# Linear attention with a multiplicative FFN on one Trainium2 core: v of batches 0 and 1 cast to bf16 by its loading DMA, and the sum of k for them by small matmuls on two columns of ones

## The chip, the core and the metric

The kernel runs on one NeuronCore of a Trainium2 chip. TensorE (PE) multiplies matrices into PSUM; VectorE (DVE), ScalarE (ACT) and GpSimd (POOL) do the elementwise work; SyncE (SP) and POOL issue the transfers between HBM and the on-chip memory (SBUF), each on its own DMA queue, SP's called q1 and POOL's q0 in the profile. The metric is the device time of one execution in microseconds (us), lower is better, given as the median of several runs.

## The reference

There are 8 batches, 8 heads, 576 positions and a head dimension of 64. Attention is linear: q and k go through phi, k and v are summed over the positions into a 64x64 matrix per head, k alone is summed into a vector, and each q row is multiplied by both. The result, 4608 rows of 512, goes through an FFN of which the two last matrices follow each other with nothing between.

```python
phi = lambda x: np.where(x > 0, x, np.exp(x) - 1.0) + 1.0
q_p, k_p = phi(q), phi(k)
kv  = np.einsum('bhsd,bhse->bhde', k_p, v)
z   = np.sum(k_p, axis=2)
num = np.einsum('bhsd,bhde->bhse', q_p, kv)
den = np.einsum('bhsd,bhd->bhs', q_p, z)[..., None] + 1e-06
x   = (num / den).transpose(0, 2, 1, 3).reshape(4608, 512)
out = ((x @ w1) * (x @ w2) @ w3) @ w_out
```

## The kernel before

**Order.** The whole program is a list of steps written out by hand, the string `ORDER`. Each step is a letter, a batch or chunk number and a part; the steps are issued in that order, and every engine and every queue executes what it got in that order. A `+` after a step moves it to another engine: loads go to POOL's queue instead of SP's, copies to DVE instead of ACT.

**Attention.** Per batch, 512 of the 576 positions are laid out with four positions (`j`) to a partition, in two halves of four heads; the last 64 positions are a tail of their own. Steps `L`, `M`, `N` load a half of k, q and v as f32 into one of 13 shared `ld` buffers (line 95, 512 KB each), `R` loads the tails (line 104). The steps x, y and z (X, Y, Z for q) make phi of k: exp on ACT (line 168), max and add (line 173) and a min (line 198, line 193 for the tail) on DVE. The step `v` casts a half of v to bf16 (line 204) or its tail (line 210). The target of the cast is `vts[b % 2]`, laid out position, head, 65 columns: 64 of v and a last one that holds 1.0, written once by POOL in the steps `I1` and `I2` (line 84). So the step `K` (lines 216 to 235) gets the sum of k with the product: a matmul over two heads has 2 x 65 = 130 moving columns, and there are 16 of them in a batch (line 225), and two more of 260 columns for the tail (line 229), all accumulating in one PSUM bank per head pair. The result is copied to `kv` (line 234). Step `A` multiplies q by it (line 280) and divides (lines 284 to 286); for batches 0 and 1 the transposes of q (`a`, line 257) and of x (`P`, line 301) run on PE, and only the tails of q of these batches go through a DMA transpose (`T1.1`, `T0.1`, line 249, on SP).

**FFN.** The loads of the weights (`B`, `C`, `E`; lines 114, 118, 126) are issued by POOL and cast f32 to bf16 on the way. Since W3 and W_out follow each other, steps `w` and `u` (lines 136 and 143) multiply them into one matrix at the start. After that a chunk of 512 rows is eight `F` steps (lines 322 to 328, 8 matmuls of 512 columns each, ACT copies one product, DVE multiplies it by the other) and four `O` steps (line 479), stored by `S` (line 489).

The part of the order that the change touches is at the start. Steps on v of batches 0 and 1: loads `N0.1+ N0.0+ N1.0+ N1.1+` on POOL; casts `v0.1` on ACT and `v0.0+ v1.0+ v1.1+` on DVE; tails `v0.2+` on DVE and `v1.2` on ACT; then `K0` and `K1+`.

Of the kernel before, what the change touches and what calls it, by code (L numbers as in the profile page):

```python
# [9 lines left out]
BF16 = mybir.dt.bfloat16  # L10
# [3 lines left out]
P = 128  # L14
# [6 lines left out]
def kernel(  # L21
# [11 lines left out]
    nc = tc.nc  # L33
    B, H, S, D = q.shape
# [35 lines left out]
    vts = [wpool.tile([P, NJ, H, E1], BF16, name=f"vt{i}") for i in range(2)]  # L70
# [3 lines left out]
    def copy_of(alt):  # L74
        return (nc.scalar.copy, nc.vector.tensor_copy, nc.gpsimd.tensor_copy)[alt]

    def constants(part, alt):
        if part == 0:
            make_identity(nc, ident)
        else:  # L80
            eng = nc.vector if alt else nc.gpsimd
            for t in (vrs[part - 1], kvs[part - 1]):
                eng.memset(t, 0.0)
            eng.memset(vts[part - 1][..., D:E1], 1.0)
            for g in range(2):
                eng.memset(vrs[part - 1][g * R:(g + 1) * R, :, g, :, D:E1], 1.0)

# [128 lines left out]
    def kv_full(b, alt):  # L216
        kj, kr = ph["k", b]
        vt, vr, kv = vts[b % 2], vrs[b % 2], kvs[b % 2]
        kvp = at_ps.tile([P, 2, NCH], F32, tag="at", name="kvp")
        W = 2 * E1  # L220
        for i in range(2):
            for g in range(2):
                hp = 2 * g + i
                for j in range(NJ):
                    nc.tensor.matmul(kvp[:, i, g * W:(g + 1) * W],  # L225
                                     kj[:, hp, j].rearrange("p u d -> p (u d)"),
                                     vt[:, j, 2 * hp:2 * hp + 2, :].rearrange("p h e -> p (h e)"),
                                     start=(g == 0 and j == 0), stop=False, skip_group_check=True)
            nc.tensor.matmul(kvp[:, i, 0:2 * W], kr[:, i * P:(i + 1) * P],  # L229
                             vr[:, i].rearrange("p g u e -> p (g u e)"),  # L230
                             start=False, stop=True, skip_group_check=True)
        for u in range(2):
            rows = slice(u * D, (u + 1) * D)
            copy_of(alt)(out=kv[rows, :, :, u], in_=kvp[rows, :, 0:2 * W].rearrange(
                "p i (g u e) -> p i g u e", g=2, u=2)[:, :, :, u])
# [283 lines left out]

    ORDER = """  # L520
    M0.0+ Y0.0 C1 E0 M0.1 I0 X0.0 E3 X0.1 L0.0 Y0.1 Z0.0 Z0.1 C0 y0.0 w0+ R0.0 R0.1 x0.0 E4 x0.2 I1
    w3+ L0.1+ x0.1 a0.0+ E1 y0.2 a0.1+ N0.1+ u0.2+ N0.0+ z0.0 R1.1 v0.1 y0.1 w4+ u3.2+ E2 w1+ z0.2
    z0.1 v0.0+ u4.2 E5 L1.0+ E7 v0.2+ E6 K0 M1.0+ M1.1+ w2 A0.3 y1.0 x1.0 L1.1+ u1.2 A0.0 w5 R1.0+
    u2.2+ w6 A0.2 B3.0 P0.3 Y1.0 z1.0 u5.2 I2 B3.1 X1.0 A0.1 w7+ P0.0 X1.1 Y1.1 N1.0+ N1.1+ Z1.0
    u6.2+ x1.2 P0.2+ x1.1 y1.2 P0.1 u7.2 Z1.1 y1.1 z1.1 B1.0 a1.0+ B1.1 v1.0+ B2.0 B2.1 F0.6 B0.0
    v1.1+ z1.2 T1.1 T0.1 v1.2 F0.7 M2.1 a1.1 K1+ F0.2 A1.2 F0.3 A1.3 F0.4 B0.1 A1.0 P1.2 F0.5 P1.3
    L2.1 A1.1 P1.0+ X2.1 R2.0+ h0 h1 A0.4 P1.1+ Y2.1 h2 h3 R3.0+ M3.1 i0 A1.4 M2.0 i1 x2.1 X3.1 Z2.1
    F1.7 F1.6 x2.2 L2.0 y2.1 y2.2 Y2.0 x3.2 R3.1+ X2.0 O0.3 N2.1 x2.0 z2.1 N2.0 y2.0 z2.2 Z2.0 F1.0
    M3.0 R5.0+ y3.2 T2.0 v2.1 L3.0 Y3.1 R2.1+ F1.5 N3.1 v2.0+ z2.0 L3.1 Z3.1 v2.2+ O0.2 F1.2 F1.1
    Y3.0 y5.2 z3.2 K2 F1.4 A2.2 X3.0 F1.3 L4.0 A2.3 x3.0 O0.1 Z3.0 A2.0 x3.1 N3.0 y3.0 O0.0 v3.1  # L530
    S0.1 A2.1 y3.1 R5.1+ z3.0 z3.1 v3.0 v3.2 O1.1+ O1.0 T3.0 D2.0 S0.0 K3 R4.1+ R4.0+ O1.3 A3.0 O1.2
    A3.2 L4.1 v4.2+ F2.6 A3.3 F2.3 N4.1 y4.1 F2.1 M4.0 x4.1 A3.1 x4.0 F2.0 M4.1 y4.2 M6.1 v5.2+ x4.2
    F2.7 Y4.0 D3.0 F2.4 z4.1 X4.1 F2.2 Y4.1 v4.1 S1.0 F2.5 Z4.1 M5.0 N4.0 X4.0 Z4.0 A3.4 z4.2 y4.0
    O2.3 F3.7 M5.1 Y5.0 v4.0 A2.4 F3.6 z4.0 L5.0 T4.0 R6.0+ x5.2 Y5.1 X5.0 F3.1 N5.1 Z5.0 S1.1 O2.2+
    K4 F3.2 M6.0 x6.2 X5.1 A4.2 Z5.1 F3.4 z5.2 F3.5 y5.0 A4.1 F3.0 L5.1 F3.3 N5.0 y5.1 X6.1 y6.2
    O2.1 A4.3 R6.1+ N6.0 S2.1 x5.1 N6.1 v5.0+ T5.0 O2.0 x5.0 v5.1+ A4.0 R7.0+ z5.1 D4.0 z5.0 X6.0
    O3.3 y7.2 O3.2+ K5+ S2.0 L6.0 z6.2 O3.1 A5.2 L6.1 O3.0 A5.1 D1.1 Y6.1 Z6.1 F4.2 A5.0 Y6.0 F4.5
    y6.1 F4.7 v6.0+ x6.1 L7.0 x6.0 M7.0 A5.3 D3.1 x7.0 z6.1 F4.0 v6.1+ v6.2 F4.6 A4.4 Z6.0 F4.1 S3.0
    F4.4 D5.0 A5.4 y6.0 z6.0 F4.3 M7.1 F5.7 x7.2 y7.0 Y7.0 z7.2 L7.1 N7.0 K6+ z7.0 F5.6 F5.0 y7.1
    X7.1 X7.0 Z7.0 F5.5 S3.1 F5.3 Y7.1 T6.0 R7.1+ Z7.1 A6.3 T7.0 F5.1 O4.2 A6.1 x7.1 O4.1 A6.2 N7.1  # L540
    z7.1 F5.4 A6.0 F5.2 v7.1 v7.2+ O4.0 D6.0 D5.1 A6.4 v7.0 O4.3+ S4.1 K7 O5.0 F6.3 S4.0 O5.1 A7.4
    F6.5 F6.4 D7.1 F6.1 A7.3 O5.2 O5.3 A7.1 F6.2 F8.3 A7.0 F8.6 S5.1 F6.6 A7.2 S5.0 F6.0 F6.7 D7.0
    O6.3+ O6.2 O6.1 O6.0+ F7.1 F7.7 F7.2 F8.0 S6.1 F8.7 S6.0 F8.1 F8.5 F7.4 F8.2 F8.4 F7.6 O8.2 F7.5
    H8.2 F7.3 F7.0 O8.3 H8.3 O7.0 O7.1 S7.0 O8.0 O8.1 S8.0 O7.2 H7.2 Q7.3
    """
    GATES = ""
    ctx.enter_context(tc.manual_schedule())
# [8 lines left out]
    def step(s):  # L556
# [106 lines left out]
```

## Time and profile before

| What | Value |
|---|---|
| median of 3 runs | 257.89 us (257.8, 257.89, 259.88) |
| the profiled execution | 259.98 us, of which the profile's span is 256.4 us |
| TensorE clock granted | 0.998 |
| matmuls and weight loads in the records | 1352 and 1368 |
| HBM read and written | 38.80 MB and 9.44 MB |
| casts of v, f32 to bf16, 128x1024 | 8 on ACT at 1050 ns, 8 on DVE at 691 ns (median; 685 to 929) |
| loads of v issued on POOL | 4 of 512 KB, 10.0 us from issue to landing (median) |

The span begins with the first instruction and ends with the last; the profiled execution has 3.6 us beside it. In the profile a line such as `L225 PE MATMUL kvp<-vt,kj` names the source line, the engine, the operation, and the tiles written and read. An idle time in brackets is put down to whatever came last. Matmuls are pipelined: a matmul of 512 columns is listed with 379 ns, but the next one starts 216 ns later, and eight of 130 columns start 56 ns apart (eight in 0.45 us in the chain of waits).

### The profile page before, as it was taken

Reading aid. Unit: us, or ns where it says so; the run is one execution under the profiler, and the core shown is the slowest. Engines: PE = TensorE matmul, PEld = TensorE weight load, DVE = VectorE, ACT = ScalarE, POOL = GpSimd, SP = SyncE. Lnnn points to the kernel's source line nnn. Section 1 sums busy time; section 2 is a strip of 40 time slices with the busy share of each in tenths; the row PEclk is TensorE's granted clock in tenths of the full one; section 3 lists DMA queues with packets and bytes.
Section 4 is the critical chain, followed back from the end, with each engine's and each line's share of the span. In section 5 each row is a group of like instructions: output and inputs, shape, how many; then the busy total and the mean of one; then the engine's idle time right before and its main releaser. Section 6 shows DMA issues by size and latency. Waiting matters only on the chain.

```text
span 256.4 us, 3789 instructions
## 1 busy us (share of the span) xinstructions
PE 231.0 (90%) x1352; PEld 117.0 (46%) x1368; DVE 159.1 (62%) x350; ACT 117.1 (46%) x180; POOL 48.8 (19%) x84
## 2 busy tenths in 40 slices
PE   0087999999999859999999999999999999999994
PEld 0063665554454424445445445444544444444442
DVE  0548589777998525997887899987244642432300
ACT  2404677247756605756553383544423223233231
POOL 8634479364044300410000000000000000000000
PEclk9999999999999999999999999999999999999999
DMA  6999999999999999799999989736710343000144
GB/s 221 211 238 286 306 261 247 204 229 285 307 239 293 220 213 324 187 289 257 310 355 206 292 246 261 196 63 150 230 20 32 134 83 164 0 3 0 41 143 144
DMA packets 63890, 50.57 MB, mean 197 GB/s; under 512 B 33536, under 2 KB 58368, under 8 KB 63872
## 3 DMA queue, kind: packets, MB, share of 16 engines
q1 hardware_dynamic: 54576, 37.10, 57.2%
q0 software_dynamic: 9152, 13.11, 22.9%
q8 instruction: 10, 0.16, 0.3%
q10 hardware_dynamic: 144, 0.13, 0.1%
q14 instruction: 8, 0.07, 0.1%
HBM read 38.80 MB, written 9.44 MB: 188 GB/s over the span
## 4 chain that ended last, share of the span: by engine, by line
PE 68%; DMA 20%; DVE 4%; issue 3%; SPq 1%; POOL 1%; ACT 1%; DVEq 0%; ACTq 0%; POOLq 0%
PE b_ps L322 22%; PE a_ps L322 22%; PE o_ps L479 18%; DMA w3b<-in_moe_w_dram 9%; DMA out_dram<-o_sb 7%; DMA qk32r<-in_k_dram 3%; PE nd L280 3%; PE kvp L225 2%; SPq L311 1%; DVE y L173 1%; PE o_ps L504 1%; DVE vt L204 1%; ACT a_sb L327 1%; PE kvp L229 1%; DVE kj L198 1%
## 5 line engine op out<-in xcount | busy, mean ns | idle before, releaser
L322 PEld LDWEIGHTS <-w_sb 128*128 128x128 bf16 x576 | 55.1, 98 | 62.8 <-issue 1.6
L328 DVE TENSOR_TENSOR ab<-a_sb,b_ps 128x512 bf16<-128x512 f32 x72 | 49.0, 685 | 39.2 <-PE b_ps L322 28.5
L322 PE MATMUL a_ps<-xt,w_sb 128*128 128x512 bf16 x256 | 66.7, 379 | 0.7 <-ACT a_sb L327 0.6
L322 PE MATMUL b_ps<-xt,w_sb 128*128 128x512 bf16 x256 | 66.7, 379 | 0.2 <-ACT a_sb L327 0.2
L327 ACT COPY a_sb<-a_ps 128x512 f32<-128x512 f32 x72 | 41.8, 586 | 53.1 <-PE a_ps L322 48.7
L479 PE MATMUL o_ps<-wf_sb,ab 128*128 128x512 bf16 x267 | 62.7, 379 | 0.8 <-issue 0.2
L479 PEld LDWEIGHTS <-ab 128*128 128x128 bf16 x280 | 26.9, 98 | 29.9
L481 ACT COPY o_sb<-o_ps 128x512 f32<-128x512 f32 x29 | 16.8, 586 | 43.8 <-PE o_ps L479 33.4
L286 DVE TENSOR_TENSOR xn<-nd,r 128x512 bf16<-128x512 f32 x32 | 22.1, 691 | 1.1
L168 ACT ACTIVATE e<-q 128x1024 bf16<-128x1024 f32 x16 | 16.7, 1055 | 9.4 <-DMA q<-in_q_dram 9.4
L168 ACT ACTIVATE e<-k 128x1024 bf16<-128x1024 f32 x16 | 16.6, 1055 | 4.8 <-DMA k<-in_k_dram 4.8
L280 PE MATMUL nd<-kv,qt 128*128 128x130 bf16 (+1 forms) x160 | 15.8, 220 | 3.1 <-DMA qt<-qj 2.6
L280 PEld LDWEIGHTS <-qt 128*128 128x128 bf16 (+1 forms) x160 | 11.3, 99 | 14.4 <-DMA qt<-qj 3.1
L136 PE MATMUL w3p<-ident,w3b 128*128 128x128 bf16 x64 | 5.7, 242 | 13.2 <-DMA w3b<-in_moe_w_dram 13.2
L284 DVE TENSOR_SCALAR r<-nd 128x8 f32<-128x8 f32 (+1 forms) x40 | 6.4, 161 | 16.2 <-PE nd L280 15.8
L173 DVE TENSOR_SCALAR y<-q 128x1024 bf16<-128x1024 f32 x16 | 11.0, 693 | 7.9 <-DMA q<-in_q_dram 7.9
L143 PE MATMUL wf_ps<-wt_sb,w3t 128*128 128x512 bf16 x61 | 14.8, 379 | 0.8 <-DMA wt_sb<-in_moe_w_out_dram 0.7
L104 POOL DMA_DIRECT2D qk32r<-in_q_dram x14 | 9.0, 648 | 19.2 <-ACT a_sb L327 17.9
L225 PE MATMUL kvp<-vt,kj 128*128 128x130 bf16 x128 | 9.8, 219 | 2.8 <-DVE vt L204 2.0
L198 DVE TENSOR_TENSOR qj<-e,y 128x512 bf16<-128x512 bf16 x32 | 11.9, 416 | 0.4 <-ACT e L168 0.3
L204 ACT CAST vt<-v 128x1024 bf16<-128x1024 f32 x8 | 8.4, 1050 | 7.9 <-DMA v<-in_v_dram 7.9
L198 DVE TENSOR_TENSOR kj<-e,y 128x512 bf16<-128x512 bf16 x32 | 11.9, 418 | 0.2
(54 smaller groups left out, 176.4 us busy)
## 6 DMA issues: line engine op xcount, KB each, us to landing
out_dram<-o_sb SPq DMA_DIRECT2D x15, 512.0 KB, 3.5
q<-in_q_dram SPq DMA_DIRECT2D x13, 512.0 KB, 8.5
k<-in_k_dram SPq DMA_DIRECT2D x13, 512.0 KB, 6.5
v<-in_v_dram SPq DMA_DIRECT2D x12, 512.0 KB, 8.1
w3b<-in_moe_w_dram POOLq DMA_DIRECT2D x8, 256.0 KB, 12.1
v<-in_v_dram POOLq DMA_DIRECT2D x4, 512.0 KB, 10.0
w_sb<-in_moe_w_dram POOLq DMA_DIRECT2D x8, 256.0 KB, 7.1
q<-in_q_dram POOLq DMA_DIRECT2D x3, 512.0 KB, 11.5
```

The costliest lines, as they stand in the source:

```text
L143: nc.tensor.matmul(wfs[i], w3ts[i][:, kc, :], wo_sb[:, kc, :], start=(kc == 0), stop=(kc == FC - 1))
L168: nc.scalar.activation(out=e, in_=x, func=AF.Exp)
L173: (nc.gpsimd if alt else nc.vector).tensor_scalar(out=y, in0=x, scalar1=0.0, scalar2=1.0, op0=ALU.max, op1=ALU.add)
L198: nc.vector.tensor_tensor(out=p[0][:, 2 * g + c].rearrange("p j u d -> p u j d"), in0=e[:, c], in1=y[:, c], op=ALU.min)
L225: nc.tensor.matmul(kvp[:, i, g * W:(g + 1) * W], kj[:, hp, j].rearrange("p u d -> p (u d)"), vt[:, j, 2 * hp:2 * hp + 2, :].rearrange("p h ...
L280: nc.tensor.matmul(nd[rows, g, i * 2 * E1:(i + 1) * 2 * E1], w, kvs[b % 2][:, i, g].rearrange("p u e -> p (u e)"), start=True, stop=True)
L286: nc.vector.tensor_tensor(out=dst.rearrange("p (g h) e -> p g h e", g=2), in0=v4[:, :, :, 0:D], in1=r[rows].unsqueeze(3).to_broadcast([n, ...
L322: nc.tensor.matmul(ps, w[:, kc, f * P:(f + 1) * P], xt_of(c)[:, :, kc, :], start=(kc == 0), stop=(kc == KC - 1))
L327: nc.scalar.copy(out=a_sb, in_=a_ps)
L328: nc.vector.tensor_mul(out=abs_[c][:, f, :], in0=a_sb, in1=b_ps)
L479: nc.tensor.matmul(o_ps, ab[:, f, m * P:(m + 1) * P], wf_sb[:, f, :], start=(f == 0), stop=(f == FC - 1))
L481: copy_of(alt)(out=rows_of(c, m // 2)[:, m % 2], in_=o_ps)
```

## The change

The loads of v of batches 0 and 1 (`N0.*`, `N1.*`) no longer go to an `ld` buffer as f32. They are issued on POOL as before, but write bf16 straight into `vts[b]`, cast on the way, in another layout: head, position, 64 columns without gaps (`v_plain`). The four casts `v0.1`, `v0.0+`, `v1.0+`, `v1.1+` are gone from the order. As this layout has no column of ones, each of the 16 matmuls of `K0` and of `K1+` becomes two with the same weights: one over the 2 x 64 columns of v, and one over two columns of a constant tile `ones`, which writes the two columns of the sum. The column of ones for the later batches is written by DVE in two new steps, `I3` after `K0` and `I4` after `K1+`; `ones` is set by DVE in `I0`. The tails, and all batches from 2 on, are as they were.

```diff
+    ones = consts.tile([P, 2], BF16)
...
     def constants(part, alt):
         if part == 0:
             make_identity(nc, ident)
+            nc.vector.memset(ones, 1.0)
+        elif part > 2:
+            nc.vector.memset(vts[part - 3][..., D:E1], 1.0)
         else:
...
-            eng.memset(vts[part - 1][..., D:E1], 1.0)
...
+    def v_plain(b):
+        return vts[b % 2].rearrange("p j h e -> p (j h e)")[:, 0:JW].rearrange("p (h x) -> p h x", x=NJ * D)
+
     def load_qkv(name, b, g, alt):
+        if name == "v" and b < 2:
+            return nc.gpsimd.dma_start(
+                out=v_plain(b)[:, 4 * g:4 * g + 4],
+                in_=src[name][b, 4 * g:4 * g + 4, 0:NJ * P, :].rearrange("h (p j) d -> p h (j d)", j=NJ))
...
                 for j in range(NJ):
+                    if b < 2:
+                        o4 = kvp[:, i, g * W:(g + 1) * W].rearrange("p (u e) -> p u e", e=E1)
+                        kw = kj[:, hp, j].rearrange("p u d -> p (u d)")
+                        nc.tensor.matmul(o4[:, :, 0:D], kw,
+                                         v_plain(b)[:, 2 * hp:2 * hp + 2, j * D:(j + 1) * D],
+                                         start=(g == 0 and j == 0), stop=False, skip_group_check=True)
+                        nc.tensor.matmul(o4[:, :, D:E1], kw, ones.unsqueeze(2),
+                                         start=False, stop=False, skip_group_check=True)
+                        continue
```

In the order, with only the steps around each edit (the line breaks are shifted by it throughout):

```diff
-    ... N0.0+ z0.0 R1.1 v0.1 y0.1 w4+ u3.2+ E2 w1+ z0.2 z0.1 v0.0+ u4.2 E5 L1.0+ E7 v0.2+ E6 K0 M1.0+ ...
+    ... N0.0+ z0.0 R1.1 y0.1 w4+ u3.2+ E2 w1+ z0.2 z0.1 u4.2 E5 L1.0+ E7 v0.2+ E6 K0 I3 M1.0+ ...
-    ... B1.0 a1.0+ B1.1 v1.0+ B2.0 B2.1 F0.6 B0.0 v1.1+ z1.2 T1.1 T0.1 v1.2 F0.7 M2.1 a1.1 K1+ F0.2 ...
+    ... B1.0 a1.0+ B1.1 B2.0 B2.1 F0.6 B0.0 z1.2 T1.1 T0.1 v1.2 F0.7 M2.1 a1.1 K1+ I4 F0.2 ...
```

More of the change, by code (lines that the diff above doesn't have):

```diff
@@ L521 @@
     M0.0+ Y0.0 C1 E0 M0.1 I0 X0.0 E3 X0.1 L0.0 Y0.1 Z0.0 Z0.1 C0 y0.0 w0+ R0.0 R0.1 x0.0 E4 x0.2 I1
[L522 to L541, printed above, removed]
@@ L542 @@
-    F6.5 F6.4 D7.1 F6.1 A7.3 O5.2 O5.3 A7.1 F6.2 F8.3 A7.0 F8.6 S5.1 F6.6 A7.2 S5.0 F6.0 F6.7 D7.0
-    O6.3+ O6.2 O6.1 O6.0+ F7.1 F7.7 F7.2 F8.0 S6.1 F8.7 S6.0 F8.1 F8.5 F7.4 F8.2 F8.4 F7.6 O8.2 F7.5
-    H8.2 F7.3 F7.0 O8.3 H8.3 O7.0 O7.1 S7.0 O8.0 O8.1 S8.0 O7.2 H7.2 Q7.3
+    w3+ L0.1+ x0.1 a0.0+ E1 y0.2 a0.1+ N0.1+ u0.2+ N0.0+ z0.0 R1.1 y0.1 w4+ u3.2+ E2 w1+ z0.2 z0.1
+    u4.2 E5 L1.0+ E7 v0.2+ E6 K0 I3 M1.0+ M1.1+ w2 A0.3 y1.0 x1.0 L1.1+ u1.2 A0.0 w5 R1.0+ u2.2+ w6
+    A0.2 B3.0 P0.3 Y1.0 z1.0 u5.2 I2 B3.1 X1.0 A0.1 w7+ P0.0 X1.1 Y1.1 N1.0+ N1.1+ Z1.0 u6.2+ x1.2
@@ new lines @@
+    P0.2+ x1.1 y1.2 P0.1 u7.2 Z1.1 y1.1 z1.1 B1.0 a1.0+ B1.1 B2.0 B2.1 F0.6 B0.0 z1.2 T1.1 T0.1 v1.2
+    F0.7 M2.1 a1.1 K1+ I4 F0.2 A1.2 F0.3 A1.3 F0.4 B0.1 A1.0 P1.2 F0.5 P1.3 L2.1 A1.1 P1.0+ X2.1
+    R2.0+ h0 h1 A0.4 P1.1+ Y2.1 h2 h3 R3.0+ M3.1 i0 A1.4 M2.0 i1 x2.1 X3.1 Z2.1 F1.7 F1.6 x2.2 L2.0
+    y2.1 y2.2 Y2.0 x3.2 R3.1+ X2.0 O0.3 N2.1 x2.0 z2.1 N2.0 y2.0 z2.2 Z2.0 F1.0 M3.0 R5.0+ y3.2 T2.0
+    v2.1 L3.0 Y3.1 R2.1+ F1.5 N3.1 v2.0+ z2.0 L3.1 Z3.1 v2.2+ O0.2 F1.2 F1.1 Y3.0 y5.2 z3.2 K2 F1.4
@@ new lines @@
+    A2.2 X3.0 F1.3 L4.0 A2.3 x3.0 O0.1 Z3.0 A2.0 x3.1 N3.0 y3.0 O0.0 v3.1 S0.1 A2.1 y3.1 R5.1+ z3.0
+    z3.1 v3.0 v3.2 O1.1+ O1.0 T3.0 D2.0 S0.0 K3 R4.1+ R4.0+ O1.3 A3.0 O1.2 A3.2 L4.1 v4.2+ F2.6 A3.3
+    F2.3 N4.1 y4.1 F2.1 M4.0 x4.1 A3.1 x4.0 F2.0 M4.1 y4.2 M6.1 v5.2+ x4.2 F2.7 Y4.0 D3.0 F2.4 z4.1
+    X4.1 F2.2 Y4.1 v4.1 S1.0 F2.5 Z4.1 M5.0 N4.0 X4.0 Z4.0 A3.4 z4.2 y4.0 O2.3 F3.7 M5.1 Y5.0 v4.0
+    A2.4 F3.6 z4.0 L5.0 T4.0 R6.0+ x5.2 Y5.1 X5.0 F3.1 N5.1 Z5.0 S1.1 O2.2+ K4 F3.2 M6.0 x6.2 X5.1
@@ new lines @@
+    A4.2 Z5.1 F3.4 z5.2 F3.5 y5.0 A4.1 F3.0 L5.1 F3.3 N5.0 y5.1 X6.1 y6.2 O2.1 A4.3 R6.1+ N6.0 S2.1
+    x5.1 N6.1 v5.0+ T5.0 O2.0 x5.0 v5.1+ A4.0 R7.0+ z5.1 D4.0 z5.0 X6.0 O3.3 y7.2 O3.2+ K5+ S2.0
+    L6.0 z6.2 O3.1 A5.2 L6.1 O3.0 A5.1 D1.1 Y6.1 Z6.1 F4.2 A5.0 Y6.0 F4.5 y6.1 F4.7 v6.0+ x6.1 L7.0
+    x6.0 M7.0 A5.3 D3.1 x7.0 z6.1 F4.0 v6.1+ v6.2 F4.6 A4.4 Z6.0 F4.1 S3.0 F4.4 D5.0 A5.4 y6.0 z6.0
+    F4.3 M7.1 F5.7 x7.2 y7.0 Y7.0 z7.2 L7.1 N7.0 K6+ z7.0 F5.6 F5.0 y7.1 X7.1 X7.0 Z7.0 F5.5 S3.1
@@ L545 @@
+    F5.3 Y7.1 T6.0 R7.1+ Z7.1 A6.3 T7.0 F5.1 O4.2 A6.1 x7.1 O4.1 A6.2 N7.1 z7.1 F5.4 A6.0 F5.2 v7.1
+    v7.2+ O4.0 D6.0 D5.1 A6.4 v7.0 O4.3+ S4.1 K7 O5.0 F6.3 S4.0 O5.1 A7.4 F6.5 F6.4 D7.1 F6.1 A7.3
+    O5.2 O5.3 A7.1 F6.2 F8.3 A7.0 F8.6 S5.1 F6.6 A7.2 S5.0 F6.0 F6.7 D7.0 O6.3+ O6.2 O6.1 O6.0+ F7.1
+    F7.7 F7.2 F8.0 S6.1 F8.7 S6.0 F8.1 F8.5 F7.4 F8.2 F8.4 F7.6 O8.2 F7.5 H8.2 F7.3 F7.0 O8.3 H8.3
+    O7.0 O7.1 S7.0 O8.0 O8.1 S8.0 O7.2 H7.2 Q7.3
     """
```

## The prediction, made before the changed kernel ran

> **What bounds the kernel now.** I read the page's shares and slices first, then who waits on PE, then the chain of waits, the time line around `K0` and `K1`, and the transfer rate in short stretches. The slices:
>
> ```profile
> PE   0087999999999859999999999999999999999994
> ...
> DMA  6999999999999999799999989736710343000144
> ```
>
> A slice is 6.41 us. PE is nearly full from the fifth slice on (25.6 us), but for slices 14 and 15 (83 to 96 us). The DMA engines are full from slice 2 to slice 16 (about 102 us) and, after a break, to slice 24 (154 us); but behind 100 us PE waits for them no more, as the next answers show. So the first 100 us belong to both, the rest to PE alone. PE's waits, first those from 28.1 to 47 us, then those from 47 us to the end:
>
> ```profile
> PE nd L280 <- ACT kv L234: 0.5, 1, 0.5
> PE kvp L225 <- DVE vt L204: 0.4, 1, 0.4
> ```
>
> ```profile
> PE nd L280 <- DMA qt<-qj: 2.6, 1, 2.6
> PE kvp L225 <- ACT vt L204: 0.8, 1, 0.8
> PE a_ps L322 <- ACT a_sb L327: 0.6, 1, 0.6
> PE b_ps L322 <- ACT a_sb L327: 0.2, 1, 0.2
> PE o_ps L479 <- issue: 0.2, 1, 0.2
> ```
>
> The columns are total us, times, longest. Before 47 us, what waits for v costs PE something just ahead of each `K`. After 47 us there are about 4.4 us, most of it at 87 to 100 us and owed to transfers: a DMA transpose, a cast waiting for v, ACT held up by a full store buffer. The chain of waits agrees; here it goes through the start and then through that stretch (start, us, what):
>
> ```profile
> 29.90 8.18 DMA qk32r<-in_k_dram
> ...
> 42.74 0.93 DVE vt L204
> 44.18 0.80 DVE vt L204
> 45.02 0.39 PE kvp L225 x4
> ...
> 75.05 12.37 DMA out_dram<-o_sb
> ```
>
> So DMA sets the pace until 38 us, DVE's casts of v stand in front of `K1`, and DMA again until about 100 us. The time line shows both `K` steps waiting for a cast:
>
> ```profile
> 25.52 0.63 PE L225 MATMUL kvp<-vt,kj 128*128 128x130 bf16 x8 [1.54 <-DVE vt L204]
> ...
> 26.82 0.27 PE L229 MATMUL kvp<-vr,qj 128*128 128x260 bf16 x1
> ...
> 28.00 0.39 PE L280 MATMUL nd<-kv,qt 128*128 128x130 bf16 x4 [0.46 <-ACT kv L234]
> ```
>
> **The loads.** Four transfers keep their place on POOL's queue and their issue; only their writing changes. The price of a plain and of a casting transfer, from stretches where one kind fills the queue (plain 32 to 34 and 39 to 41 us, the casting loads of W1 and W2 36 to 38 and 46 to 49 us; the last two columns are DMA share and GB/s written):
>
> ```profile
> 32.00:34.00 2.00, 2.00 (x23) 1.41 (x22) 1.38 (x4) 1.00 (x2) 1.68 (x3) 1.00 1.03 350
> 36.00:38.00 2.00, 2.00 (x17) 1.08 (x15) 2.00 (x4) 2.00 (x3) 0.48 (x2) 1.00 1.48 198
> 39.00:41.00 2.00, 2.00 (x17) 1.15 (x16) 2.00 (x6) 1.72 (x3) 2.00 (x4) 1.00 1.03 359
> 46.00:49.00 3.00, 3.00 (x20) 1.52 (x18) 1.79 (x5) 0.59 (x1) 1.23 (x2) 1.00 1.46 196
> ```
>
> A half of v is 524288 B plain: 1.46 to 1.50 us at 350 to 359 GB/s. Cast it writes 262144 B: 1.32 to 1.34 us at 196 to 198. The loads of W1 and W2 are the right neighbour, since each of their rows is 256 f32, 1 KB, as a row of v is. So a cast costs about what it reads, and the four save 4 x 0.15 = 0.6 us. Bounds: the busy share counts against it, 1.33 us x 1.47 = 1.95 against 1.48 x 1.03 = 1.52, +0.43 each, +1.7 in all, if the share and not the rate is what others feel; the fastest casting stretch (24 to 26 us, W3 in rows of 4 KB, 212 GB/s) gives 1.24 us and -1.0 in all. I take -0.6, the nearest row. POOL's issue of a plain v takes 0.76 us (median) and that of a W1 load the same 0.76 at 32.29, so nothing changes there; POOL also loses two memsets of 0.27 us, but what it issues there joins a queue that is already full. [...]
>
> **K0.** Its inputs: the second half of v lands at 24.77 us (DVE's cast starts there after 0.78 us of waiting for it); the cast ends at 25.47 and PE starts at 25.52. Without the cast PE starts at 24.8, and DVE, free from 23.98 (end of the step before), can do the tail cast ahead of it, which removes PE's 0.27 us for that. Each of the 16 matmuls brings a small one with its own weight load. No row shows a matmul of two columns. Below nothing is excluded, since instructions are only added; the lower bound is about 0, if two columns cost their share of the 130 and the load stays hidden; the upper is 98 ns, the weight load's own duration in line 225's group, if nothing hides it. I take 56 ns, the spacing of load and matmul pairs in the same group, because the load must still happen and has only a tiny matmul to hide behind. So 16 x 112 + 2 x 110 = 2.01 us, and the last L229 starts at 24.8 + 1.90 = 26.70 instead of 26.82: -0.1 us for `nd` at 28.00. PE has no gap worth naming from there to `K1`, so this -0.1 is carried along. [...]
>
> **K1.** PE reaches it at 44.18 us, issues four matmuls and waits until 45.02; `F0.2` starts at 46.03. Without waits the step takes 2.01 us, so `F0.2` would start at 44.18 + 2.01 = 46.19: +0.16, less the 0.1 from before. The second half of v1 arrives on POOL's queue ahead of 42.7 us (the cast of its first half starts at 42.74, the second's at 44.18, neither waits for a transfer), 1.5 us ahead of need. At 47 us PE is thus +0.06.
>
> **DVE, ACT, SP.** DVE is rid of casts of 0.70, 0.93 and 0.79 us and ACT of 1.05. That ACT cast waited for the DMA and nobody waited behind it for more than 0.3 us. DVE's two at 42.74 and 44.18 stood before `z1.2` (44.88), on which SP's queue hung: SP issues nothing between 10.4 and 45.32 us, where `T1.1` starts. It can now start at about 43.9, and behind it the loads of batch 2 (first at 47.93) come 1.4 us earlier. As the engines are full with POOL's transfers until 50 us, this shifts the order of the transfers more than their sum: I count 0 for it, and the full 1.4 us as a rival. The three new memsets on DVE (128x32, 128x32, 128x2) cost some 0.16 us each, the row of `r` with 8 columns (the same fill on POOL took 0.27). `ones` falls before an idle time of 2.29 us (13.58); `I3` waits for `K0`'s last read, with the divisions of `A0.3` behind it, inside an idle time of 2.23 us (28.43); `I4` comes after the copy of `kv` (ends 47.17), with the product of `F0.2` behind it, which waited 0.86 us for PE (48.03). Without that cover they cost 0.16 to 0.27 each. Four fewer `ld` buffers are taken, but those that batch 2 reuses have been free since batch 0.
>
> **Sum.** PE alone: +0.06 us at 47 us. Then the stretch at 87 to 100 us, where PE waits for transfers that left after the four loads and behind a queue that never ran dry: -0.6 there, of which I take 0.5, since part of these waits hangs on DVE and PE. PE's +0.06 falls into that wait. What follows is PE work, unchanged. Against its own execution: span 256.4 - 0.5 = 255.9, run 259.98 - 0.5 = 259.5. That execution was 2.1 us above the median of the runs, so I predict 257.89 - 0.5 = 257.4.
>
> **Rivals.**
> 1. *SP's early start goes through* (faster). The loads of batch 2 and so the waits at 87 to 100 us come 1.4 us earlier on top of the 0.5: 256.0; if the waits after 47 us vanish altogether, 4.4: 253.5. For it: SP is idle for 35 us before `T1.1`. Against it: full engines. Chance 0.20.
> 2. *Bytes written count* (faster). 262144 B at 350 GB/s are 0.75 us instead of 1.50, -0.75 x 4 = -3.0: 254.9. It decides if the casts of v exceed 300 GB/s written; the rows at 196 speak against it. [...] Chance 0.04.
> 3. *The busy share counts* (slower). Smaller packets hold the engines longer: +1.7 in the queue, half of it already at 38.16 us, where ACT waits for k's tail and `F0.6` hangs on ACT with 0.06 us to spare; the other half in the later waits: 259.6. If it also sets back the transposes and stores at 87 to 100 us by as much again, 261.3. It decides if k's tail lands later than 38.16. Chance 0.18.
> 4. *The weight loads show* (slower). 98 ns for each small pair: `K0` +0.57 after its 0.1 gain, `K1` +0.16 + 16 x 0.042 = +0.83: with both carried to the end 259.3. Against it: the waits at 87 to 100 us would swallow some. Chance 0.10.
> 5. *The change doesn't do what it says*: the small matmuls cost more waits than the casts did, or v arrives last anyway, and PE still starts `K` where it did. Then K costs 0.9 twice, and the end +0.5 to +1.3: inside 1%. Chance 0.08.
>
> **Chances.** The forecast, from -1.3 to +0.5, has the remaining 0.40. 1% is 2.6 us, about what a measurement of this kernel can tell. Over 1% faster: rival 2 and half of 1, 0.14. Over 1% slower: a good half of 3 with its knock-on, and 3 and 4 together, 0.15. Within: 0.71. The range leaves out the far ends of 1 and 2 and of 3: 255.0 to 260.5.
>
> **What would show it.** Right: no cast of v before batch 2; `K0` starting near 24.8 and `K1` without a gap, each 2.0 us long; pairs 112 ns apart; written rate near 196 GB/s while v loads; `T1.1` near 43.9 us; the wait for `qt` at 87 to 93 us shorter by half a microsecond. Wrong: k's tail landing after 38.5 us, pairs 150 ns apart, or a new wait of PE between 28 and 47 us.

## The result, and the profile after

The changed kernel takes 257.05 us (median of 17 runs, 255.3 to 259.5), the kernel before 258.7 us beside it (17 runs, 257.33 to 260.57). The ratio is 0.9945, with a 95% interval of 0.9923 to 0.9967: 1.4 us less, between 0.85 and 2.0. That is a small gain: the interval leaves out 1, but the change stays under the 1% that the prediction set as its mark.

The profiled execution of the changed kernel took 255.3 us, the shortest of its 17, with a span of 253.5 us. The two spans (256.4 and 253.5) are thus 2.9 us apart, where the ratio stands for 1.4 us and the medians are 1.65 apart: about half of what the two traces show is spread between executions. A second trace of the changed kernel, taken later (`e12_changed_again`), has a span of 254.5 us; it too is of the shortest execution of its series (256.28 us of 8), while the trace of the kernel before is of a long one (259.98 us). I trust a difference only if both traces of the changed kernel show it, and even then its size is too large.

PE's and the DMA engines' slices of the changed kernel, from its page:

```profile
PE   0088999999999789999999999999999999999994
...
DMA  6999999999999999899999989646611244000144
```

PE's hole at 83 to 96 us is shallower (slices 14 and 15 were 8 and 5, and are 7 and 8, at 6.34 us a slice). PE's waits, first from 28.1 to 47 us, then from 47 us to the end (total us, times, longest):

```profile
PE a_ps L341 <- ACT xt L321: 0.6, 1, 0.6
PE w3p L146 <- DMA w3b<-in_moe_w_dram: 0.2, 1, 0.2
```

```profile
PE kvp L244 <- ACT vt L214: 1.4, 1, 1.4
PE a_ps L341 <- DMA xt<-xn: 0.8, 1, 0.8
```

Behind 47 us PE waits for 2.2 us instead of 4.4; in the second trace it is 3.0. Ahead of 47 us the wait for the cast of v has gone, and another has come in its place, for ACT's copy of `xt`. The time line says why (start, us, engine and line, what; in brackets the idle time before it and what ended it):

```profile
24.70 0.22 PE L238 MATMUL kvp<-vt,kj 128*128 128x128 bf16 x1 [0.59 <-DMA vt<-in_v_dram]
24.76 0.17 PE L241 MATMUL kvp<-ones,kj 128*128 128x2 bf16 x1
24.79 0.22 PE L238 MATMUL kvp<-vt,kj 128*128 128x128 bf16 x1
24.84 0.17 PE L241 MATMUL kvp<-ones,kj 128*128 128x2 bf16 x1
...
27.30 0.39 PE L299 MATMUL nd<-kv,qt 128*128 128x130 bf16 x4 [0.46 <-ACT kv L253]
...
38.48 0.63 ACT L178 ACTIVATE er<-qk32r 128x512 bf16<-128x512 f32 x1 [0.70 <-DMA qk32r<-in_k_dram]
...
39.97 0.56 ACT L321 COPY xt<-xtp 128x512 bf16<-128x512 bf16 x1
...
40.58 1.02 PE L341 MATMUL a_ps<-xt,w_sb 128*128 128x512 bf16 x4 [0.56 <-ACT xt L321]
```

`K0` starts at 24.70 us instead of 25.52, and `nd` follows 0.7 us earlier. But the first `F` starts at 40.58 us (40.28 before): its `xt` is copied by ACT behind two exponentials, and the first of these waits for the tail of k, which lands when the queue brings it (ACT starts on it at 38.48 us against 38.18; at 38.12 in the second trace, with its first `F` at 40.22). So PE's 0.7 us is lost at 40 us. By 58.5 us the two kernels are about level: the 64th matmul of `F` starts at 58.54 us before and at 58.52 after (58.16 in the second trace). The 128th is 0.6 us ahead (78.15 and 77.59; 77.23 in the second trace), the 160th 2.8 (103.31 and 100.51; 101.31). From there to the end of the span 11 of the 14 traces of this study need 153.0 to 153.4 us; `e7`, `e8` and `e10` need 154.3 to 155.3. **Between these traces the gain thus arises from 58 to 103 us, where nothing was changed.**

What reaches that stretch from the change is SP's queue. SP's transposes of q and x, before the change (the first row is `T1.1` and `T0.1`; then `T3.0` and `D2.0`):

```profile
45.32 2.57 SPq L249 DMA_TRANSPOSE qt<-qj  x2
...
81.09 6.24 SPq L249 DMA_TRANSPOSE qt<-qj  x1
...
87.42 4.25 SPq L311 DMA_TRANSPOSE xt<-xn  x1
```

and after it:

```profile
43.63 2.74 SPq L268 DMA_TRANSPOSE qt<-qj  x2
...
80.54 6.90 SPq L268 DMA_TRANSPOSE qt<-qj  x1
...
87.53 1.87 SPq L330 DMA_TRANSPOSE xt<-xn  x1
```

SP starts 1.7 us earlier, as DVE has two casts less in front of `z1.2`. The loads of batch 2 behind it start 1.5 us earlier (46.41 instead of 47.93), `T3.0` 0.55, and `D2.0` no earlier at all; but `T3.0` lands at 89.6 us instead of 92.9, and `D2.0` at 93.3 instead of 95.3. In the chain of waits of the changed kernel that landing is what PE goes on from (start, us, what):

```profile
74.23 13.31 DMA out_dram<-o_sb
87.53 5.79 DMA xt<-xn
93.37 1.02 PE a_ps L341 x4
```

This gave the first theory, A: the gain is SP's early start. Its rivals were B, the transfers became cheaper; C, PE's own gain at `K0` and `K1`; later D and E, named below where they came up.

### The profile page after: what moved, and what is told of

The parts are those of the page before. It is cut to its first block, busy times and chain, and to the rows that moved or that the text cites. A ratio compares the mean times of both kernels' runs of the same rounds, so it can differ in the third digit from the quotient of the medians.

```text
span 253.5 us, 3863 instructions
## 1 busy us (share of the span) xinstructions
PE 231.9 (91%) x1400; PEld 118.1 (47%) x1400; DVE 156.9 (62%) x350; ACT 116.3 (46%) x179; POOL 48.9 (19%) x82
## 4 chain that ended last, share of the span: by engine, by line
PE 75%; DMA 20%; POOL 1%; issue 1%; ACT 1%; ACTq 0%; POOLq 0%
PE a_ps L341 24%; PE b_ps L341 24%; PE o_ps L498 20%; DMA w3b<-in_moe_w_dram 10%; DMA out_dram<-o_sb 5%; PE nd L299 3%; DMA qk32r<-in_k_dram 3%; DMA xt<-xn 2%; PE kvp L244 2%; PE o_ps L523 1%; PE kvp L248 1%; PE kvp L238 0%; POOL w3b L136 0%; ACT e L178 0%; PE xtp L320 0%
## 5 line engine op out<-in xcount | busy, mean ns | idle before, releaser
L498 PE MATMUL o_ps<-wf_sb,ab 128*128 128x512 bf16 x280 | 64.4, 379 | 0.0
L146 PEld LDWEIGHTS <-w3b 128*128 128x128 bf16 x64 | 4.5, 108 | 15.0 <-DMA w3b<-in_moe_w_dram 14.8
L114 POOL DMA_DIRECT2D v32r<-in_v_dram x12 | 7.6, 640 | 18.1 <-DVE vr L220 8.1
## 6 DMA issues: line engine op xcount, KB each, us to landing
w3b<-in_moe_w_dram POOLq DMA_DIRECT2D x8, 256.0 KB, 12.2
w_sb<-in_moe_w_dram POOLq DMA_DIRECT2D x8, 256.0 KB, 7.3
```

The source lines that it names most:

```text
L114: ins = (nc.gpsimd if alt else nc.sync).dma_start(out=t[g * R:(g + 1) * R, i].rearrange("p (h d) -> p h d", d=D), in_=src[name][b, g * 4:( ...
L498: nc.tensor.matmul(o_ps, ab[:, f, m * P:(m + 1) * P], wf_sb[:, f, :], start=(f == 0), stop=(f == FC - 1))
```

## The experiments

Each ratio is to the kernel before, run beside it, with its 95% interval. It is not the quotient of the two medians in its row, which differs from it by up to 0.0023 (`e11_z12_middle`: 0.9905, `e12_changed_again`: 0.9951); small differences between ratios mean little for that reason too. Most kernels ran 12 times, `e1` and `e11` only 6 times and `e12` 8 times. The table gives for each kernel also what its one trace shows: the start of `T1.1`, the issue of `L2.0` (half of k of batch 2, SP's fifth load behind `T1.1`), the landing of `D2.0`, the most that a halved TensorE clock can have cost before PE's last matmul (half of the time at half clock; explained under the last heading), and the span.

| Kernel | ratio [95%] | median us (before) | `T1.1` at | `L2.0` issued | `D2.0` lands | half clock cost at most | span |
|---|---|---|---|---|---|---|---|
| before | 1 | 258.7 | 45.32 | 51.84 | 95.3 | 0 | 256.4 |
| after | 0.9945 [0.9923, 0.9967] | 257.05 (258.7) | 43.63 | 50.59 | 93.3 | 0 | 253.5 |
| e1_dve_casts_back | 1.0090 [1.0056, 1.0124] | 260.65 (258.39) | 44.84 | 51.71 | 98.3 | 3.4 | 259.3 |
| e2_small_matmuls_only | 0.9966 [0.9939, 0.9993] | 257.74 (258.39) | 45.31 | 51.89 | 94.6 | 0 | 255.6 |
| e3_z12_early | 0.9949 [0.9921, 0.9977] | 257.02 (258.39) | 43.26 | 51.36 | 96.0 | 0 | 256.4 |
| e4_plain_loads | 0.9988 [0.9954, 1.0021] | 257.54 (258.39) | 43.53 | 51.62 | 94.6 | 0 | 255.4 |
| e5_z12_late | 1.0004 [0.9973, 1.0034] | 258.44 (258.92) | 45.00 | 51.15 | 95.5 | 0 | 256.0 |
| e6_z12_first | 1.0002 [0.9966, 1.0039] | 258.96 (258.92) | 39.96 | 48.48 | 97.2 | 1.7 | 258.7 |
| e7_batch1_only | 0.9998 [0.9963, 1.0034] | 259.05 (258.92) | 43.77 | 52.14 | 94.8 | 0 | 257.4 |
| e8_batch0_only | 1.0026 [0.9996, 1.0057] | 259.46 (258.92) | 45.15 | 51.49 | 96.2 | 1.7 | 258.8 |
| e9_batch1_again | 0.9992 [0.9960, 1.0024] | 258.3 (258.99) | 43.83 | 52.14 | 95.1 | 0 | 256.2 |
| e10_batch1_z12_late | 0.9998 [0.9968, 1.0028] | 259.13 (258.99) | 45.19 | 51.52 | 94.5 | 0 | 257.8 |
| e11_z12_middle | 0.9885 [0.9853, 0.9918] | 256.53 (258.99) | 42.40 | 50.63 | 94.2 | 1.7 | 255.0 |
| e12_changed_again | 0.9928 [0.9891, 0.9966] | 257.73 (258.99) | 43.27 | 50.39 | 93.8 | 0 | 254.5 |

**DVE's casts put back.** The changed kernel, with two casts of the same size (of q of batch 1, into a tile nobody reads) where DVE had cast v of batch 1:

```diff
+        elif t == "j":
+            nc.vector.tensor_copy(
+                out=scr[:, :, 4 * i:4 * i + 4, 0:D],
+                in_=raw["q", b, i].rearrange("p (h j d) -> p j h d", h=H // 2, j=NJ))
...
-    ... B1.0 a1.0+ B1.1 B2.0 B2.1 F0.6 B0.0 z1.2 T1.1 T0.1 ...
+    ... B1.0 a1.0+ B1.1 j1.0 B2.0 B2.1 F0.6 B0.0 j1.1 z1.2 T1.1 T0.1 ...
```

> The changed kernel with two DVE casts put back where v1.0+ and v1.1+ stood. They read q of batch 1 and write a scratch tile that nobody reads, so the loads and the matmuls stay as changed and only DVE's load at 42 to 45 us returns. Theory A (the gain comes through SP's queue, which starts T1.1 at 43.6 instead of 45.3 us because DVE reaches z1.2 earlier): T1.1 back near 45.2 us and most of the 0.55% lost, ratio to before 0.998 to 1.001. Theory B (the gain comes from the transfers being cheaper) and theory C (it comes from PE, K0 and K1 done earlier): ratio stays at 0.993 to 0.996.

`T1.1` went back to 44.84 us and the gain was gone, as A says. But the kernel is 0.9% slower than the one before, which A doesn't say. Two things ask for caution: the cast also holds a buffer of q for longer, and about half of what its trace lost is of another kind. The clock granted to PE, in stretches of 2 us (width, PE busy and weight loads with counts, DVE, ACT, POOL, then the clock, DMA share, GB/s):

```profile
88.00:90.00 2.00, 0.24 (x5) 0.24 (x5) 0.00 (x0) 1.34 (x2) 0.00 (x0) 1.00 1.30 144
90.00:92.00 2.00, 1.21 (x17) 0.90 (x15) 0.17 (x1) 0.95 (x4) 1.23 (x2) 0.83 1.32 93
92.00:94.00 2.00, 1.20 (x3) 0.55 (x4) 0.52 (x1) 0.70 (x3) 0.00 (x0) 0.50 1.21 209
94.00:96.00 2.00, 2.00 (x7) 0.64 (x5) 0.00 (x0) 0.00 (x0) 0.00 (x0) 0.50 1.33 212
```

After PE's wait of 2.4 us its clock was halved for 6.8 us, from 91.3 to 98.1 us: the matmuls of `O` in these rows start 0.43 us apart, against 0.22 at full clock. PE stood still for 1.5 us of that time, so the halving cost some 2.7 us, nearly the whole distance to the kernel before (259.3 against 256.4). The other five executions were granted a clock of 0.992 to 0.998 on average, against 0.985 in this one, and took 260.07 to 260.68 us all the same. So the halved clock does not explain why this kernel is slower than the one before; what does stays open.

**The small matmuls alone.** The kernel before, with each matmul of `K0` and `K1` split into 128 and 2 columns of the same tile:

```diff
+                        nc.tensor.matmul(o4[:, :, 0:D], kw, vt[:, j, 2 * hp:2 * hp + 2, 0:D], ...)
+                        nc.tensor.matmul(o4[:, :, D:E1], kw, vt[:, j, 2 * hp:2 * hp + 2, D:E1], ...)
```

> The kernel before with only the matmuls changed: K0 and K1 take 16 products of 2 x 64 columns and 16 of the two columns of ones, from the same vt as before; loads and casts as before. Pairs 82 ns apart as in the changed kernel instead of 56, so K0 and K1 are each 0.42 us longer. Theory C: carried to the end, ratio 1.002 to 1.004. Theories A and B: swallowed by the waits for transfers at 87 to 100 us, 0.999 to 1.002.

Its time line of `K0`:

```profile
25.47 0.22 PE L228 MATMUL kvp<-vt,kj 128*128 128x128 bf16 x1 [1.51 <-DVE vt L204]
25.52 0.17 PE L230 MATMUL kvp<-vt,kj 128*128 128x2 bf16 x1
25.55 0.22 PE L228 MATMUL kvp<-vt,kj 128*128 128x128 bf16 x1
```

A pair takes 84 ns here and 82 in the changed kernel, of which the large matmul has 56 and 55 and the small one 28 and 27. `K0` and `K1` are 0.1 to 0.2 us longer and the whole kernel is no slower, so that work on PE there does not set the end. A, B and C had all expected 0.999 or more; the ratio of 0.9966 is a miss for all of them. Its trace shows no reason, and its interval all but touches 1. It is a warning of how little a difference of 0.3% between two kernels tells here.

**SP early, without the change.** The kernel before, with only the step that SP hangs on moved ahead of DVE's two casts:

```diff
-    ... a1.0+ B1.1 v1.0+ B2.0 B2.1 F0.6 B0.0 v1.1+ z1.2 T1.1 T0.1 v1.2 ...
+    ... a1.0+ z1.2 B1.1 v1.0+ B2.0 B2.1 F0.6 B0.0 v1.1+ T1.1 T0.1 v1.2 ...
```

> The kernel before with one step moved: z1.2 goes ahead of the DVE casts v1.0+ and v1.1+, and with it SP's T1.1 and T0.1; nothing else is changed, so K1 waits 0.4 us longer for v. T1.1 should start near 43.3 us instead of 45.3. Theory A: SP's earlier start alone gives most of the gain, ratio 0.994 to 0.997. Theories B and C: no gain, 0.999 to 1.003.

0.9949 against the change's 0.9945: one moved step gives what the change gave, with all casts in place. For A; against B and C. But `e2_small_matmuls_only` beside it, with SP late, is only 0.0017 behind, and the two intervals overlap widely, so this is weak support. Its trace is a long execution (258.17 us, median 257.02) and does not show the gain, so that only the times speak here.

**Plain loads.** The changed kernel, loading v as f32 into the `ld` buffers again, while the matmuls read the upper half of each f32 as bf16 (v is cut off, not rounded), so that no cast is needed:

```diff
-                out=v_plain(b)[:, 4 * g:4 * g + 4],
+                out=t.rearrange("p (h x) -> p h x", x=NJ * D),
...
+        t = raw["v", b, hp // 2].bitcast(BF16).rearrange("p (h x two) -> p h x two", two=2, x=NJ * D)
+        return t[:, 2 * (hp % 2):2 * (hp % 2) + 2, j * D:(j + 1) * D, 1]
```

> The changed kernel with the four loads of v as plain f32 transfers into ld buffers as before; the matmuls read the upper halves of the f32 numbers as bf16 (so v is cut off rather than rounded), columns 4 bytes apart. No casts on any engine, the transfers as before. Theory B: the gain of the cheaper transfers, 0.6 us by my estimate, is lost: ratio about 0.0025 above the changed kernel's, 0.997. Theories A and C: the same as the changed kernel, 0.993 to 0.996. If PE reads columns 4 bytes apart more slowly, the pairs in K0 show it.

Inconclusive: the interval overlaps both that of the change and 1. With SP early (43.53 us), A had expected 0.993 to 0.996; 0.9988 is nearer to no gain. The matmuls that read columns 4 bytes apart are hardly slower (85 ns a pair, against 82). The landings are clearer. The second half of v of batch 1 lands at 43.3 us here, in the changed kernel and in the kernel before alike, that of batch 0 at 25.0, 24.7 and 24.7 us. From the landing of a first half to that of its second it takes 1.36 and 1.33 us with the cast, and 1.45 and 1.36 us in the kernel before. The casting load is at most 0.1 us shorter than the plain one; the two traces of the changed kernel are further apart than that (43.26 and 42.69 us for the last half).

**SP late, with the change.** The changed kernel, with `z1.2 T1.1 T0.1` put back by about what DVE's casts had cost:

```diff
-    ... F0.6 B0.0 z1.2 T1.1 T0.1 v1.2 F0.7 M2.1 ...
+    ... F0.6 B0.0 v1.2 F0.7 z1.2 T1.1 T0.1 M2.1 ...
```

> The changed kernel with one step moved: z1.2, and SP's T1.1 and T0.1 with it, go behind the product of F0.7 on DVE, which puts T1.1 back to about 45.4 us. No load and no cast added, PE's order unchanged. Theory A (SP's earlier start is the gain): ratio 0.998 to 1.002. Theories B and C (cheaper transfers, PE earlier): 0.993 to 0.996. Theory D (the run with the DVE casts put back lost for another reason than SP's start, its scratch tile or the DVE load): also 0.993 to 0.996.

SP's first transposes, and PE's longest waits after 47 us:

```profile
45.00 2.56 SPq L268 DMA_TRANSPOSE qt<-qj  x2
```

```profile
PE kvp L244 <- ACT vt L214: 2.1, 1, 2.1
PE a_ps L341 <- DMA xt<-xn: 0.8, 1, 0.8
PE nd L299 <- DMA qt<-qj: 0.4, 1, 0.4
```

The gain is gone, with the casting loads, the small matmuls and the early `K0` all in place, and the interval does not overlap the changed kernel's: B and C fall as causes of the whole gain, and so does D, by which the casts put back had lost the gain for another reason than SP's start (the further 0.9% that they cost stays open). A small part can't be excluded: the prediction's 0.5 us would be a ratio of 0.998, inside this interval. The moved step takes `z1.2` itself along on DVE, and its place there and SP's start were not tried apart. Together with `e3_z12_early`, A has both directions, the second of them clearly: what starts SP early seems to make the gain without the change, and what starts it late takes the gain out of the change.

**SP as early as it can.** The same three steps right behind `y1.2 P0.1 u7.2`:

```diff
-    ... y1.2 P0.1 u7.2 Z1.1 ... F0.6 B0.0 z1.2 T1.1 T0.1 v1.2 ...
+    ... y1.2 P0.1 u7.2 z1.2 T1.1 T0.1 Z1.1 ... F0.6 B0.0 v1.2 ...
```

> The changed kernel with z1.2, T1.1 and T0.1 moved ahead of Z1.1, to right behind y1.2 and the last product of the weights: T1.1 should start near 40 us instead of 43.6, and the loads of batch 2 near 43. Theory A by dose: a further 1 to 2 us, ratio 0.986 to 0.992, unless the loads of W1 and W2, which PE needs from 46 us on, come late beside them (then PE waits at F0.2 or F0.4 and the ratio is 0.995 or more). Theories B and C: no change from 0.9945.

SP's transposes start at 39.96 us, and batch 2's loads with them. They now run among the last loads of W1 and W2, of which the last lands at 58.2 us instead of 53.9. The time line of PE there:

```profile
58.23 0.39 PE L341 MATMUL b_ps<-xt,w_sb 128*128 128x512 bf16 x1 [2.44 <-DMA w_sb<-in_moe_w_dram]
```

So SP's transfers start 3.7 us earlier here than in the changed kernel (43.63 us) and the last of W1 and W2 lands 4.3 us later, at a DMA share of 1.23 to 1.29 from 48 to 55 us. In this trace half clock after that wait (59.1 to 62.5 us) cost up to 1.7 us more.

**One batch alone.** The change for batch 1 only (`if b == 1` in place of `if b < 2`, the casts `v0.1` and `v0.0+` back in their places, the column of ones of batch 0 set by POOL again), and for batch 0 only (likewise, with `v1.0+` and `v1.1+` back):

```diff
-        if name == "v" and b < 2:
+        if name == "v" and b == 1:
```

> The change for batch 1 alone: v of batch 0 is loaded as f32 and cast as before, K0 as before; the two DVE casts before K1 are gone and T1.1 starts near 43.6 us. Theory A: the whole gain, 0.993 to 0.997. Theory B: half of it, about 0.997. Theory C: no gain from K0; K1's small matmuls cost what its wait did, 1.000.

> The change for batch 0 alone: K0 0.7 us earlier, two casting loads, but the DVE casts of v of batch 1 stay, so T1.1 stays near 45.3 us. Theory A: no gain, 0.998 to 1.002. Theory B: half of it, about 0.997. Theory C: most of it, 0.994 to 0.997.

Batch 0 alone gains nothing, and SP starts late in it (45.15 us): as A has it. Batch 1 alone starts SP at 43.77 us, as early as the change, and gains nothing either: a clear miss for A. So the early start alone doesn't give the gain. Theory E came from this: it needs SP's early start, but the end also hangs on how the transfers of 45 to 60 us fall. I ran the kernel for batch 1 again, and with SP late:

```diff
-    ... F0.6 B0.0 z1.2 T1.1 T0.1 v1.2 F0.7 M2.1 ...
+    ... F0.6 B0.0 v1.2 F0.7 z1.2 T1.1 T0.1 M2.1 ...
```

> The change for batch 1 alone, a second time: the first gave 0.9998 although T1.1 started early, where theory A wanted 0.993 to 0.997. If that was the spread between executions, 0.994 to 0.998 now; if batch 1 alone lacks something (theory E: SP's start is necessary but the end also hangs on how the transfers at 45 to 60 us fall), 0.998 to 1.001 again.

> The change for batch 1 alone, with z1.2 and T1.1 put back behind the product of F0.7, so that SP starts at about 45.4 instead of 43.8 us; nothing else is moved. Theories A and E: slower than the same without the move by 0.004 to 0.006 (1.002 to 1.006). Theories B and C: the same as it.

The first stays at 1, as E expected. The second is not measurably slower, although its SP starts at 45.19 us: both A and E had expected 1.002 to 1.006, so 0.9998 is a miss for E too. (The medians, 258.3 and 259.13 us, are 0.8 us apart the expected way; the ratios are 0.0006 apart, with intervals of 0.003 to each side.) To what these runs can tell, the start of SP is worth nothing with batch 1 alone. SP's queue shows one place where its lead goes. Its loads of batch 2 in `e9_batch1_again`, first two, then a pair of q, then `L2.0` (start, us that SP spends on them):

```profile
46.83 0.65 SPq L107 DMA_DIRECT2D q<-in_q_dram  x1
47.52 0.52 SPq L107 DMA_DIRECT2D k<-in_k_dram  x1
48.08 3.96 SPq L107 DMA_DIRECT2D q<-in_q_dram  x2
52.14 2.14 SPq L107 DMA_DIRECT2D k<-in_k_dram  x1
```

and in the changed kernel:

```profile
47.05 0.54 SPq L105 DMA_DIRECT2D k<-in_k_dram  x1
47.64 2.91 SPq L105 DMA_DIRECT2D q<-in_q_dram  x2
50.59 2.58 SPq L105 DMA_DIRECT2D k<-in_k_dram  x1
```

The pair of q holds SP for 4.0 us, against 2.9 in the changed kernel, so that `L2.0` goes out at 52.14 us in both traces of this kernel: later than where SP started 1.4 us later (51.52 in `e10_batch1_z12_late`, 51.84 before). So one part of E is borne out, that the end hangs on more than SP's start: the lead is there at 46.8 us and gone at 52.1. Across the table `L2.0`, picked after the fact, sorts the kernels better than `T1.1` does: both traces of the changed kernel and `e11_z12_middle` have it below 51 us, all others, but for `e6_z12_first` with its price elsewhere, above, `e4_plain_loads` among them at 51.62. It doesn't sort them all: `e3_z12_early` gains at 51.36 and `e5_z12_late` does not at 51.15, and `e2_small_matmuls_only` at 51.89 has its small gain (each has one trace, and that of `e3` is a long execution). Later, too, these kernels differ. PE's longest wait behind 47 us is for a cast of v in the changed kernel and ends at 87 us; in `e7` to `e10` it ends at 90 to 91 us and is for DVE's copy into the store buffer, which waits for SP's first store (in `e9_batch1_again`):

```profile
89.74 0.69 DVE L502 COPY o_sb<-o_ps 128x512 f32<-128x512 f32 x1 [4.25 <-DMA out_dram<-o_sb]
```

That store lands at 89.65 us in `e9_batch1_again` and at 87.62 and 88.16 in the changed kernel; but at 87.42 in the kernel before, so it is not what makes the gain. Why SP is held longer at that pair of loads when v of batch 0 comes by plain loads was not tried and stays open.

**SP in between.** `z1.2 T1.1 T0.1` right behind `z1.1`, and in the same series the changed kernel itself once more:

```diff
-    ... y1.1 z1.1 B1.0 a1.0+ B1.1 B2.0 B2.1 F0.6 B0.0 z1.2 T1.1 T0.1 v1.2 ...
+    ... y1.1 z1.1 z1.2 T1.1 T0.1 B1.0 a1.0+ B1.1 B2.0 B2.1 F0.6 B0.0 v1.2 ...
```

> The changed kernel with z1.2, T1.1 and T0.1 right behind z1.1, so that T1.1 starts near 42.2 us, between the changed kernel (43.6) and the run with 40.0, which lost at 58 us what it had won. Theory A: if the loads of W1 and W2 for F0.0 still land before 54.6 us, as good as the changed kernel or better, 0.990 to 0.995; if they come late, PE waits ahead of h0 and the ratio is 0.996 to 1.000.

> The changed kernel as it is, for its spread and a second trace: 0.992 to 0.997. The recorded trace was the fastest of its 17 executions; one nearer the median should show more of PE's waits at 87 to 100 us (3.5 us there now), about 1.5 us more.

With SP's transposes at 42.40 us the kernel takes 256.53 us (6 runs), 0.9885 of the kernel before; its wait for W1 or W2 is back in small:

```profile
PE kvp L244 <- ACT vt L214: 2.0, 1, 2.0
PE b_ps L341 <- DMA w_sb<-in_moe_w_dram: 0.4, 1, 0.4
```

This is the best of the kernels tried, clearly ahead of the one before. Against the changed kernel beside it (257.73 us, 0.9928) the medians are 1.2 us apart and the intervals overlap, so that the further gain is likely, not certain. The second trace of the changed kernel is not the one nearer the median that was hoped for (256.28 us, the shortest of its 8); PE's waits behind 47 us are 0.8 us longer in it than in the first (3.0 and 2.2 us; the 3.5 us named above is not what the first trace lists).

**What the runs settle.** Of the orders with the whole change in them, `T1.1` at 45.0 us gives 1.0004, at 43.6 and 43.3 us 0.9945 and 0.9928, at 42.4 us 0.9885, at 40.0 us 1.0002: on these figures earlier is better until W1 and W2 come late, though the runs are few and the interval of 0.9928 overlaps its neighbours on both sides. That the change needs SP's early start for its gain is shown by undoing it (`e5_z12_late`). That the early start is enough is not shown: `e3_z12_early` speaks for it weakly, and `e7_batch1_only`, `e9_batch1_again` and perhaps `e4_plain_loads` start SP as early and gain nothing clear. With batch 1 alone the lead is gone at `L2.0`; whether that is the reason was not tried. How the lead becomes 1.4 us at the end is not shown either: between `T3.0` and the landing of `D2.0` the traces differ by more than SP's starts do.

## Why the prediction was right or wrong

The median of 257.05 us lies inside 255.0 to 260.5 and 0.35 us under the 257.4, and the change is within 1%, as the likeliest case had it. That the median came so near is partly luck: the forecast change was -0.5 us and the measured one is -1.4, but the kernel before, from whose 257.89 us (3 runs) the forecast started, took 258.7 us beside the changed one. And the reason for the change was mostly another.

- **The loads: no gain.** The price of a casting load was right: 200 GB/s written while v loads (22 to 24 us), or 1.31 us for a half, against 1.32 to 1.34. The step that failed is the saving, "the four save 4 x 0.15 = 0.6 us" carried to the waits at 87 to 100 us. From one half's landing to the next a cast takes 0.03 to 0.09 us less than a plain load, not 0.15, and the last half lands where it landed; with SP late no gain is measured (`e5_z12_late`, though 0.5 us lies inside its interval). 0.15 us was the difference of two rates read from stretches of 2 and 3 us in a shared queue, finer than such rows go.
- **SP's queue: the step that was wrong.** "I count 0 for it, and the full 1.4 us as a rival." `T1.1` was to come at 43.9 us and came at 43.63 and 43.27. Without that early start there is no gain (`e5_z12_late`), and the prediction had given it to rival 1 with a chance of 0.20. The measured 1.4 us lies between the forecast's 0.5 and that rival's 1.9. The argument for 0, that the engines are full until 50 us and the order of transfers shifts more than their sum, overlooked that the order is worth something: the last of W1 and W2 lands 0.5 to 0.9 us later in the changed kernel (53.55 and 53.94 us against 53.04) and PE doesn't wait for it, while the waits at 86 to 94 us are for transfers that come later on the queues. `e6_z12_first` shows where that argument begins to hold.
- **K0: mis-sized.** The start of 24.8 us was right (24.70). A small pair took 27 ns, not 56, so `K0` is 1.5 us long, not 2.0, and `nd` 0.7 us earlier, not 0.1. It was worth nothing all the same, since "no gap worth naming from there to `K1`" did not hold for a PE that comes early: it stands at `F0.6` until ACT has copied `xt`, behind the landing of k's tail. The new wait there, 0.5 to 0.6 us in both traces, is of the kind that the prediction had named as a sign against it; it ate PE's lead.
- **K1: right but for the size.** No wait in it, and 1.54 us instead of 2.01. "PE +0.06 at 47 us" is -0.02 at 58.5 us.
- **The cover for the small work: right.** The memsets of `I3` and `I4` take 0.09 us each, inside idle time of DVE, and nothing waits for them.
- **Rival 2, bytes written:** 200 GB/s written, not over 300. It fell. **Rival 3, the busy share:** the share is 1.47 while v loads, as reckoned, and ACT takes up k's tail at 38.48 us in one trace of the changed kernel and at 38.12 in the other, once behind the deciding 38.16 and once ahead of it, with no lengthening of the whole; not borne out. **Rival 4, the weight loads:** pairs at 82 ns, neither 112 nor 150; they don't show. **Rival 5:** `K` starts early and without a gap; it fell.
- **What was not in it:** PE's clock was at half after a wait at 87 to 100 us in three traces (for 6.8 us in `e1`, for 3.4 us each in `e8` and `e11`), so that the wait cost more than its length there, some 2.7 us more in `e1` and up to 1.7 in the two others. Neither of the two traces compared first shows it there (1.00 from 86 to 96 us in both), but `e6_z12_first` does at 59 us, for 3.4 us.

## What to carry to other kernels

When an edit takes work off one engine, look first for the queue that hangs on the next step of that engine, and price that queue's earlier start by what its transfers feed, not by whether the engines are full. Here the order of transfers still decided who waited, in full DMA engines (PE stood for 2.44 us for W1 or W2 in `e6_z12_first`, where SP starts at 39.96 us, and not at all for them in the changed kernel): bring forward what is needed next, and stop where what is passed becomes late. And undo the suspected cause with everything else left in place; here one moved step told more than all parts of the change taken singly. For an effect of half a percent, a variant that should do nothing (here `e2_small_matmuls_only`) shows how large a difference the runs can make by themselves.

## What the hardware showed that was not expected

**A matmul of two columns with its own full weight load cost 27 ns** between others of 128 columns. In the changed kernel each of the 32 weight loads for such a matmul is listed with 95 to 98 ns, and those for the large ones with 97 on average. PE is listed with 0.0 us of idle time before the small ones: two loads go into a pair of 82 ns.

**PE's clock was at half for 3.4 us, or twice that, after some waits and not after others.** In `e11_z12_middle` (columns as above):

```profile
86.00:88.00 2.00, 0.05 (x2) 0.01 (x1) 0.00 (x0) 1.11 (x2) 0.00 (x0) 1.00 1.24 142
88.00:90.00 2.00, 1.87 (x19) 1.62 (x19) 0.69 (x1) 1.24 (x3) 1.03 (x2) 0.65 1.30 263
90.00:92.00 2.00, 2.00 (x6) 0.72 (x5) 0.00 (x0) 0.75 (x2) 0.19 (x1) 0.50 1.25 158
```

PE stood for 1.95 us before it. In `e12_changed_again` it stood for 1.96 us at the same place, and in the kernel before for 2.62 at 90 to 93 us, and the clock stayed at 1.00. In three traces (`e6`, `e8`, `e11`) the clock was at half for 3.4 us, which costs up to 1.7 us, and in `e1` for twice that. In `e8_batch0_only` it halved within a wait of 1.6 us (from 90 to 91 us PE is busy for 0.00 us, and the clock is 0.76 on average), shorter than the two that left it at 1.00. So the length of one wait does not tell in these traces whether the clock is halved behind it; what does is not shown.

How much the halving adds to the spread of 1 to 2% between executions of one kernel (before: 256.79 to 261.21 us in 24 runs) is only loosely seen: the granted clock of the timed executions (0.985 to 1.000 in these 24) goes with their times with a correlation of -0.23 to -0.61 in three series of the kernel before, the lower clock with the longer time.

**A transpose by DMA behind a store took very different times.** `T3.0` lands 11.8 us after its issue before the change, and 9.0 and 10.5 us after it in the two traces of the changed kernel. In all 14 traces the landing of `D2.0`, which follows it, goes with the span (correlation 0.84), at 160.2 to 163.3 us from landing to end.
